# One ring of seven PSUM banks for the last 22 steps of a two-branch attention kernel, with its last projection units and row scaling moved

## The chip, the cores and the metric

The kernel runs on one core of a Trainium2 chip. The metric is device time in microseconds (us); the median of three runs before the change is 2747.71 us (2747.64 to 2748.46). Five engines work side by side and meet through semaphores: TensorE (PE, with its weight loads, PEld), VectorE (DVE), ScalarE (ACT), GpSimd (POOL), and SyncE (SP), which issues transfers. TensorE's results land in PSUM, which has eight banks of 128 x 512 f32; a bank may be written again only when its reader is done with it.

## The reference, cut to what matters

Two attention blocks read the same `x` (2048 x 576), each with 32 heads of 18 columns; in block B all heads share one key and one value head. A gate per row mixes the two.

```python
g = _sigmoid((x * gate_w).sum(-1, keepdims=True))
a = _A_ref(x, A_wqkv, A_wo)      # 32 heads, each with its own k and v
b = _B_ref(x, B_wq, B_wk, B_wv, B_wo)   # 32 heads, one k and one v
return g * a + (1 - g) * b
# in each: scores = q k^T * 18 ** -0.5;  p = softmax(scores);  o = p v;  heads joined;  o @ wo
```

## The kernel before, in words

There are 64 units (one per head; 0 to 31 are B's, 32 to 63 are A's). A unit has 16 steps, one per 128 keys, so the kernel has 1024 steps. A step has four scores matmuls (`step_scores`, L515; 128 keys x 512 queries each, one bank each), an exponential of each on ACT (L522, into one of 14 `pt` tiles), and the matmuls of probabilities and values (`step_pv`, L528; for the last unit `last_pv`, L539), which add into the eighth bank, `acc`. The scores run ahead of the value matmuls by two steps. The maxima that the exponentials subtract are found on DVE from a second set of scores (`step_max`, L471 and L480), 22 steps (`LEAD`) ahead. So from step 1002 on no maxima are left to find; this stretch is called the tail here. In it two scores matmuls of 56 rows stand on different halves of the PE array (`SB`, `MB`) and run beside each other.

The order of all instructions is written out by hand. `emit` reads a string of letters: `s` is one scores matmul, a digit n is n quarters of a step's value matmuls, `U` is the next unit of the output projection that waits in `todo`, `V` is the next unit of the last projection (`out_last`), and `a`, `b`, `c` are the three parts of `last_sums`, which brings half of the last unit's result into the rows of the last projection: a copy out of `acc`, a transpose (L710) with the division by the sums on DVE (L713 to L718), and transposes back (L724) with a split in a high and a low part (L115 to L119). A blank-separated stretch of a string such as "ss ss ss U 6" is called a group below.

The projection has three segments. The second (`SEG`, rows 512 to 1023 of the joined heads) gives 32 units of 12 matmuls (L677), each of which ends in one DVE addition (L686); 28 of them run before step 1002, and the last four in the tail. The third, `out_proj(8, [P])`, has 32 units of three matmuls; its rows come from the last heads and are scaled by `normalise(8, at_end=True)` (L612, L117, L119) in four chunks of 512 queries. Its units for queries 0 to 511 need chunk 0, and so on; four of its units are evicted by ACT and added by POOL (L683, L684), the others by DVE. Each finished pair of units sends a block of 128 rows to the output (L690).

Seven banks serve everything but `acc`: three of the pool `ps_s`, four of the pool `ps_m`. Before the change the tail's scores take two `ps_m` and two `ps_s` banks in turn, step by step, and the units and transposes take `ps_m` banks alone.

When a unit's value matmuls are done, `head_out` copies `acc` (L551) before the next unit's first value matmul may write it, and sends the sums and rows out. `normalise` for the last rows then waits for these sums, divides, multiplies by the gate, and brings the result back spread over partitions (`R`).

Of the kernel before, what the change touches and what calls it, by code (L numbers as in the profile page):

```python
# [8 lines left out]
F32 = mybir.dt.float32  # L9
# [3 lines left out]
OP = mybir.AluOpType  # L13
# [14 lines left out]
LEAD = 22  # L28
# [14 lines left out]
def gated_mix_kernel(ctx: ExitStack, tc: tile.TileContext, xT, wall, wv, wo, out):  # L43
    nc = tc.nc
    P = 128
# [7 lines left out]
    ps_s = ctx.enter_context(tc.tile_pool(name="ps_s", bufs=3, space=PSUM))  # L53
    ps_m = ctx.enter_context(tc.tile_pool(name="ps_m", bufs=4, space=PSUM))
# [34 lines left out]
    SB, MB = 0, 64  # L89
# [23 lines left out]
    def split(src, h, l, eng_h, eng_l):  # L113
        if eng_h is nc.scalar:
            nc.scalar.activation(h, src, AF.Copy)  # L115
        else:
            eng_h.tensor_copy(h, src)  # L117
        if l is not None:
            eng_l.tensor_tensor(l, src, h.bitcast(F32), op=OP.subtract)  # L119
# [224 lines left out]
    for n in range(4 * (LEAD_T - 3)):  # L344
        mt, c, w = next(left)
# [42 lines left out]
    L = {("kd", 0): kdb}  # L388
# [59 lines left out]
    def kst(u):  # L448
        return ksb if u < H else L["ks"][(u - H) % 3]
# [46 lines left out]
                    md.rearrange("(b i) (o a f) -> o a i b f", i=32, o=1, a=2)[:, a, 0:16])  # L496

    PT = {}

    def bank(n):  # L500

# [6 lines left out]

    def step_scores(u, i, c, alone, k):

        b = SB
        ps = (ps_m if alone and k < 2 else ps_s).tile([P, 512], F32, name="pm" if alone and k < 2 else "ps")
        if alone and k % 2:
            b = MB
        nc.tensor.matmul(ps, kst(u)[b:b + 56, i * P:(i + 1) * P],  # L515
                         qs[u % 3][b:b + 56, c * 512:(c + 1) * 512], start=True, stop=True)
        PT["q"] = PT.get("q", []) + [(c, ps)]
        if alone and k == 0:
            return
        for c, ps in PT.pop("q"):  # L520
            pt = L["pt"].tile([P, 512], F32, name="pt")
            nc.scalar.activation(pt, ps, AF.Exp, scale=SCALE)  # L522
            PT[u, i, c] = pt

    def step_pv(u, i, a, b):

        for j in range(4):
            nc.tensor.matmul(acc[32 * j:32 * j + 19, a:b], v_of(u, i), PT[u, i, j][:, a:b],  # L528
                             start=(i == 0), stop=(i == 15), skip_group_check=True)
        if b == 512:  # L530
            for j in range(4):
                del PT[u, i, j]

    def last_pv(half, i, a, b):

        for j in range(4):
            pt = PT[NU - 1, i, 2 * half + j // 2]
            x = 256 * (j % 2)
# [32 lines left out]
    def last_head(t):  # L571
        return (P * t + P - 1) // DH

    def normalise(t, at_end=False):

        u0 = 0 if t == 0 else last_head(t - 1) + 1
        u1 = min(last_head(t) + 1, NU - 1)
        rows = min(P, DH * (NU - 1) - P * t)
        off = FIRST_ROW[t]
        n = (u1 - u0) * 16  # L580
        sm = L["work"].tile([P, P], F32, name="sm", bufs=1)
        dma(sm[:n, :], sum_d[u0:u1, :].rearrange("h (s f) -> (h s) f", f=P))
        gt = L["work"].tile([P, P], F32, name="gt", bufs=1)
        dma(gt[:n, :], gu_d[u0:u1, :].rearrange("h (s f) -> (h s) f", f=P))
        yield
        yield

        g = P if t >= 7 else 32
        for c in range(0, P, g):
            nc.vector.reciprocal(sm[:n, c:c + g], sm[:n, c:c + g])  # L590
            yield
        (nc.vector if at_end else nc.gpsimd).tensor_tensor(sm[:n, :], sm[:n, :], gt[:n, :], op=OP.mult)
        dma(r_d[u0:u1, :].rearrange("h (s f) -> (h s) f", f=P), sm[:n, :])
        yield
        ot = OT.pop(t)
        R = L["work"].tile([P, S], F32, name="R", bufs=1)
        if off:
            nc.gpsimd.memset(R[0:32, :], 0.0)
        for cs in (slice(0, S // 2), slice(S // 2, S)) if at_end else (slice(0, S),):
            r0 = P * t  # L600
            while r0 < P * t + rows:
                u = r0 // DH
                n = min(DH * (u + 1), P * t + rows) - r0
                dma(R[off + r0 - P * t:off + r0 - P * t + n, cs], r_d[u:u + 1, cs].to_broadcast([n, cs.stop - cs.start]))
                r0 += n
        yield
        if at_end:
            L["end"] = {"h": qs[1], "l": L["ks"][2]}
            for c in range(4):
                cs = slice(512 * c, 512 * c + 512)  # L610
                e = nc.vector if c < 2 else nc.gpsimd
                e.tensor_tensor(ot[:, cs], ot[:, cs], R[:, cs], op=OP.mult)  # L612
                split(ot[:, cs], L["end"]["h"][:, cs], L["end"]["l"][:, cs], e, e)
            return
        for c in range(4):
            cs = slice(512 * c, 512 * c + 512)
            h = L["work"].tile([P, 512], F32R, name="oh", bufs=1)
            l = L["work"].tile([P, 512], F32R, name="ol", bufs=1)
            nc.gpsimd.tensor_tensor(ot[:rows, cs], ot[:rows, cs], R[:rows, cs], op=OP.mult)
            yield  # L620
            split(ot[:rows, cs], h[:rows], l[:rows], nc.gpsimd, nc.gpsimd)
            yield
            yield
            dma(on_d[0][P * t:P * t + rows, cs], h[:rows])
            dma(on_d[1][P * t:P * t + rows, cs], l[:rows])
            yield
# [19 lines left out]
    def out_proj(t0, rows, first=False):  # L646

        nt = len(rows)
        oacc = L["oacc"]
        fin = t0 == 8  # L650
        O = {}

        def load(q):
            for x, y in enumerate("hl"):
                if fin:
                    O[q, y] = L["end"][y][:, 256 * q:256 * q + 256].rearrange("p (t s) -> p t s", t=1)
                    continue
                t = L["pool"].tile([P, nt, 256], F32R, name=f"oi{y}", bufs=2)
                dma(t, on_d[x][P * t0:P * (t0 + nt), 256 * q:256 * q + 256]
                    .rearrange("(t p) s -> p t s", p=P))  # L660
                O[q, y] = t

        load(0)
        yield
        w = WO[t0]
        for q in range(8):
            if q < 7:
                load(q + 1)
            o = {y: O[q, y] for y in "hl"}
            for s2 in range(2):  # L670
                st_ = 2 * q + s2
                for hf in range(2):
                    ops = [(o[b][:r, t, s2 * P:(s2 + 1) * P], w[a][:r, t, 288 * hf:288 * hf + 288])
                           for a, b in PRODS for t, r in enumerate(rows)]
                    fp = ps_m.tile([P, 512], F32, name="pm")
                    for n, (x, y) in enumerate(ops):
                        nc.tensor.matmul(fp[:, 0:288], x, y, start=(n == 0), stop=(n == len(ops) - 1))  # L677
                    dst = oacc[:, st_, 288 * hf:288 * hf + 288]
                    if first:
                        nc.scalar.activation(dst, fp[:, 0:288], AF.Copy)  # L680
                    elif fin and hf == 0 and st_ in ON_ACT:
                        tmp = L["work"].tile([P, 288], F32, name="tmp", tag="ol", bufs=1)
                        nc.scalar.activation(tmp, fp[:, 0:288], AF.Copy)  # L683
                        nc.gpsimd.tensor_tensor(dst, tmp, dst, op=OP.add)  # L684
                    else:
                        nc.vector.tensor_tensor(dst, fp[:, 0:288], dst, op=OP.add)  # L686
                    if fin and st_ == 15:
                        dma(out[st_ * P:(st_ + 1) * P, 288 * hf:288 * hf + 288], dst)
                    elif fin and hf:
                        dma(out[st_ * P:(st_ + 1) * P, :], oacc[:, st_, :])  # L690
                    yield
# [5 lines left out]
    def last_sums(half):  # L697
# [7 lines left out]
        else:  # L705
            nc.vector.tensor_copy(oe[:, 0:256], acc[:, cols:cols + 256])
        yield
        pt = ps_m.tile([P, 512], F32, name="pm")
        for c in range(2):
            nc.tensor.transpose(pt[:, P * c:P * c + P], oe[:, P * c:P * c + P], ident)  # L710
        pt = pt[:, 0:256].rearrange("p (c j d) -> p c j d", c=2, d=32)
# [4 lines left out]
        ps = {}  # L716
# [2 lines left out]
                                    r[:, 2 * j:2 * j + 2].unsqueeze(2).to_broadcast([P, 2, DH]), op=OP.mult)  # L719
        yield  # L720
        for k in range(2):
            ps[k] = ps_m.tile([P, 512], F32, name="pm")
            for c in range(4):
                nc.tensor.transpose(ps[k][0:DH, P * c:P * c + P], on[:, 4 * k + c, 0:DH], ident)  # L724
        for k in range(2):
# [9 lines left out]
    NSTEP = 16 * NU  # L735
# [44 lines left out]
    for v in range(16):  # L780
        if v == 11:
            max_rows(0)
        mt, c, w = next(left)
        fp = ps_s.tile([P, 512], F32, name="ps")
# [20 lines left out]
    pos = {"s": 0, "P": 0, "x": (LEAD + 2) // 2, "y": (LEAD + 2) // 2}  # L805
# [76 lines left out]
    max_rows(NU - 1)  # L882


    for ops in ["ss ss ss U 6", "ss ss ss 6"] * 2 + ["ss ss ss U 6"] * 2 + ["ss ss ss 6"] * 5 + \
            ["a ss ss ss b 6 c", "ss ss ss 6 V V", "ss ss ss 6 V V", "ss ss V V 6 V V 6"]:
        emit(ops, 1)
    assert pos["s"] == pos["P"] == 4 * NSTEP
    emit("a V b V V c")
# [35 lines left out]
```

## Time and profile before

| What | Value |
|---|---|
| median of 3 runs | 2747.71 us |
| the profiled execution's own time | 2749.25 us |
| its span, first to last instruction | 2747.3 us |
| PE busy | 2732.3 us (99%) |
| DVE busy / ACT busy / POOL busy | 2394.7 / 2444.2 / 265.5 us |
| the tail: first paired scores to the last value matmul | 2671.25 to 2729.83 us |
| last DVE addition ends | 2742.84 us |

In the profile a row of the timeline gives the start in us, the length, engine, line, operation, output and inputs, how many instructions the row merges, and in brackets how long the engine had been idle before it and who ended that. A row of waits gives the sum of such idle time, how often it came, and the longest. Matmuls overlap, so the length of a row is longer than the time until the next matmul can start; the distance between starts is what a matmul costs its queue.

### The profile page before, as it was taken

What the parts mean: (1) busy time and instruction counts of PE and PEld (TensorE: products, weight loads), DVE (VectorE), ACT (ScalarE), POOL (GpSimd) and SP (SyncE); (2) the same over time, 40 slices, a digit from 0 to 9 for tenths busy, and PEclk for the clock granted to TensorE, in tenths of its full rate; (3) what the DMA queues carried; (4) which work ended last, traced back from release to release, by engine and by line L of the source; (5) the groups of instructions that cost most, each with busy time, mean ns of one, the idle gap of its engine ahead of it and who ended that gap; (6) DMA issues with size and microseconds to landing.
All of it is one profiled execution on the core that took longest, in us unless ns stands there. A gap on an engine that the chain in (4) does not pass through costs nothing.

```text
span 2747.3 us, 60434 instructions
## 1 busy us (share of the span) xinstructions
PE 2732.3 (99%) x23536; PEld 1301.3 (47%) x23536; DVE 2394.7 (87%) x4501; ACT 2444.2 (89%) x4787; POOL 265.5 (10%) x400
## 2 busy tenths in 40 slices
PE   9999999999999999999999999999999999999998
PEld 7874444454444333333334444444444333334555
DVE  4488888888889999999999898889889999998873
ACT  4338999999999999999999999999999999998776
POOL 2371000010001000100110001000100011011001
PEclk9999999999999999999999999999999999999999
DMA  8883211222111101211133223222321232233312
GB/s 285 325 300 125 59 50 40 61 79 74 43 57 57 56 26 34 65 48 31 47 98 104 87 61 92 91 77 67 101 86 56 59 91 91 66 97 102 111 36 87
DMA packets 145954, 242.09 MB, mean 88 GB/s; under 512 B 53650, under 2 KB 99810, under 8 KB 134092
## 3 DMA queue, kind: packets, MB, share of 16 engines
q1 hardware_dynamic: 131844, 188.16, 22.5%
q0 software_dynamic: 13504, 49.88, 4.8%
q8 instruction: 185, 3.03, 0.4%
q14 instruction: 101, 0.83, 0.1%
q10 hardware_dynamic: 320, 0.20, 0.0%
HBM read 149.61 MB, written 79.78 MB: 83 GB/s over the span
## 4 chain that ended last, share of the span: by engine, by line
PE 98%; ACT 1%; DMA 0%; issue 0%; DVE 0%; SPq 0%; ACTq 0%
PE acc L528 38%; PE ps L515 32%; PE pm L471 14%; PE ps L155 7%; PE pm L677 5%; PE pm L435 2%; ACT pt L522 1%; PE acc L539 0%; DMA wst<-wall 0%; PE ps L471 0%; PE pm L515 0%; DVE oacc L686 0%; PE pm L724 0%; PE pm L201 0%; SPq L49 0%
## 5 line engine op out<-in xcount | busy, mean ns | idle before, releaser
L522 ACT ACTIVATE pt<-ps 128x512 f32<-128x512 f32 x4052 | 2131.9, 611 | 124.2 <-PE pm L471 52.8
L480 DVE TENSOR_REDUCE mx<-pm 128x1 f32<-128x512 f32 x3064 | 1939.9, 684 | 195.0 <-PE pm L471 146.2
L515 PE MATMUL ps<-qs,ksb 56*128 56x512 f32 x2688 | 901.0, 437 | 0.6 <-DVE mx L480 0.3
L471 PE MATMUL pm<-ksb,qs 54*128 54x512 f32 x2332 | 793.4, 438 | 0.0
L515 PEld LDWEIGHTS ps<-qs,ksb 56*128 56x128 f32 x2688 | 435.8, 184 | 496.8 <-ACT pt L522 467.2
L528 PE MATMUL acc<-pt,vb 128*19 128x256 f32 (+3 forms) x6656 | 580.3, 435 | 0.1
L528 PE MATMUL acc<-pt,vg 128*19 128x256 f32 (+3 forms) x6232 | 554.2, 443 | 0.0
L515 PE MATMUL ps<-qs,ksa 56*128 56x512 f32 x1364 | 453.6, 436 | 3.9 <-ACT pt L522 3.8
L471 PEld LDWEIGHTS pm<-ksb,qs 54*128 54x128 f32 x2332 | 370.7, 185 | 124.5 <-DVE mx L480 57.0
L471 PE MATMUL pm<-ksa,qs 54*128 54x512 f32 x1232 | 425.6, 438 | 0.0
L477 DVE CUSTOM_DVE_ANT_0 junk<-pm,xb 128x512 bf16<-128x512 f32 x500 | 340.2, 680 | 1.1 <-ACT xb L474 0.9
L515 PEld LDWEIGHTS ps<-qs,ksa 56*128 56x128 f32 x1364 | 218.3, 184 | 243.5 <-ACT pt L522 225.5
L474 ACT ACTIVATE xb<-pm 128x512 f32<-128x512 f32 x500 | 307.3, 615 | 0.0
L528 PEld LDWEIGHTS acc<-pt,vb 128*19 128x19 f32 x6656 | 125.7, 97 | 216.6 <-issue 193.2
L471 PEld LDWEIGHTS pm<-ksa,qs 54*128 54x128 f32 x1232 | 198.0, 184 | 56.4 <-DVE mx L480 25.8
L528 PEld LDWEIGHTS acc<-pt,vg 128*19 128x19 f32 x6232 | 119.0, 97 | 207.0 <-issue 183.0
L117 POOL CAST mh<-mt 128x32 fp32r<-128x32 f32 x64 | 13.4, 210 | 1724.3 <-DVE mt L488 1724.3
L471 PE MATMUL pm<-kdb,qs 54*128 54x512 f32 x372 | 153.5, 413 | 0.0
L161 ACT ACTIVATE phl<-ps 128x512 fp32r<-128x512 f32 x40 | 23.9, 597 | 71.5 <-PE ps L155 57.0
L155 PE MATMUL ps<-xh,wh 128*128 128x512 f32 (+1 forms) x300 | 85.4, 383 | 0.6 <-ACT xh L274 0.3
L155 PE MATMUL ps<-xh,wl 128*128 128x512 f32 (+1 forms) x300 | 83.3, 376 | 0.0
L167 DVE TENSOR_TENSOR phl<-ps,phl 128x512 fp32r<-128x512 f32 x40 | 27.7, 692 | 62.7 <-ACT phl L161 47.2
(128 smaller groups left out, 1450.7 us busy)
## 6 DMA issues: line engine op xcount, KB each, us to landing
qs<-qk SPq DMA_DIRECT2D x384, 144.0 KB
qk<-phl POOLq DMA_DIRECT2D x56, 512.0 KB, 5.4
ksa<-qk SPq DMA_DIRECT2D x132, 144.0 KB
ksb<-qk SPq DMA_DIRECT2D x66, 144.0 KB
xv<-x_d SPq DMA_DIRECT2D x16, 576.0 KB
onh<-oh SPq DMA_DIRECT2D x32, 256.0 KB
onl<-ol SPq DMA_DIRECT2D x32, 256.0 KB
oih<-onh SPq DMA_DIRECT2D x16, 512.0 KB
```

Source lines behind the costliest of these rows:

```text
L155: nc.tensor.matmul(fp[:, p0:p0 + g], w[a][:kr, k, :], X[b][:kr, k, x0 + p0:x0 + p0 + g], start=(n == 0), stop=(n == len(PROJ) - 1))
L161: nc.scalar.activation(hl[:, 0, :], fp, AF.Copy)
L167: nc.vector.tensor_tensor(hl[:, 1, :], fp, hl[:, 0, :].bitcast(F32), op=OP.subtract)
L435: nc.tensor.matmul(fp[:, 0:288], x[:kr, k if b == "h" else NKT + k, :], w[hf][a][:kr, k, :], start=(n == 0), stop=(n == len(PROJ) - 1))
L471: nc.tensor.matmul(pm, qs[u % 3][b:b + 54, i * P:(i + 1) * P], k, start=True, stop=True)
L474: nc.scalar.activation(MX["x", u, i], pm, AF.Relu)
L477: nc.vector.tensor_tensor_reduce(junk, pm, MX.pop(("x", u, i)), 1.0, -3e38, op0=OP.add, op1=OP.max, accum_out=MX[u][:, i, c:c + 1])
L480: nc.vector.tensor_reduce(MX[u][:, i, c:c + 1], pm, axis=AX.X, op=OP.max)
L515: nc.tensor.matmul(ps, kst(u)[b:b + 56, i * P:(i + 1) * P], qs[u % 3][b:b + 56, c * 512:(c + 1) * 512], start=True, stop=True)
L522: nc.scalar.activation(pt, ps, AF.Exp, scale=SCALE)
L528: nc.tensor.matmul(acc[32 * j:32 * j + 19, a:b], v_of(u, i), PT[u, i, j][:, a:b], start=(i == 0), stop=(i == 15), skip_group_check=True)
L677: nc.tensor.matmul(fp[:, 0:288], x, y, start=(n == 0), stop=(n == len(ops) - 1))
```

## The change

Up to step 1002 the order of the instructions stays the same on every engine. From there on:

- A function `ring` hands out banks in the order s, m, s, m, s, m, m, so that scores, the second segment's last units, `last_sums` and the third segment's units all go round the same seven banks.
- The four `U` stand in groups 1, 4, 5 and 8 (counted from 0) and not in groups 0, 2, 4 and 5. Group 4 takes eight quarters of value matmuls and group 5 four, so that unit 62 ends with group 4. Group 10 has four scores and four quarters, and is followed by `a`. The eight `V` of the tail stand two each behind groups 12, 13 and 14 and one each before the last two stretches of four quarters.
- `normalise` at the end does all four chunks on POOL; before, DVE did chunks 0 and 1.

SP's order of transfers is the same. POOL gets six instructions more and DVE six fewer.

```diff
+    RING = [0]
+    def ring():
+        RING[0] += 1
+        m = RING[0] % 7 % 2
+        return (ps_m if m == 0 else ps_s).tile([P, 512], F32, name="ps" if m else "pm")
+
+    def unit_bank():
+        return ring() if pos["s"] > 4 * (NSTEP - LEAD) else ps_m.tile([P, 512], F32, name="pm")
...
     def step_scores(u, i, c, alone, k):
-        b = SB
-        ps = (ps_m if alone and k < 2 else ps_s).tile([P, 512], F32, name="pm" if alone and k < 2 else "ps")
-        if alone and k % 2:
-            b = MB
+        b = MB if alone and k % 2 else SB
+        ps = ring() if alone else ps_s.tile([P, 512], F32, name="ps")
...
             for c in range(4):
                 cs = slice(512 * c, 512 * c + 512)
-                e = nc.vector if c < 2 else nc.gpsimd
-                e.tensor_tensor(ot[:, cs], ot[:, cs], R[:, cs], op=OP.mult)
-                split(ot[:, cs], L["end"]["h"][:, cs], L["end"]["l"][:, cs], e, e)
+                nc.gpsimd.tensor_tensor(ot[:, cs], ot[:, cs], R[:, cs], op=OP.mult)
+                split(ot[:, cs], L["end"]["h"][:, cs], L["end"]["l"][:, cs], nc.gpsimd, nc.gpsimd)
...
-                    fp = ps_m.tile([P, 512], F32, name="pm")
+                    fp = unit_bank()
...
-        pt = ps_m.tile([P, 512], F32, name="pm")
+        pt = ring()
...
-            ps[k] = ps_m.tile([P, 512], F32, name="pm")
+            ps[k] = ring()
...
-    for ops in ["ss ss ss U 6", "ss ss ss 6"] * 2 + ["ss ss ss U 6"] * 2 + ["ss ss ss 6"] * 5 + \
-            ["a ss ss ss b 6 c", "ss ss ss 6 V V", "ss ss ss 6 V V", "ss ss V V 6 V V 6"]:
+    for ops in ["ss ss ss 6", "ss ss ss U 6", "ss ss ss 6", "ss ss ss 6", "ss ss ss U 8", "ss ss ss U 4",
+                "ss ss ss 6", "ss ss ss 6", "ss ss ss U 6", "ss ss ss 6", "ss ss 4 a", "ss ss ss b 6 c"] + \
+            ["ss ss ss 6 V V"] * 3 + ["V 4 V 4"]:
         emit(ops, 1)
```

## The prediction

> **What bounds the kernel now.** The page comes first, for its engines and its costliest groups; then the waits between 2671 and 2735 us, the only stretch that the change touches; then the chain that ended last; then the timelines of PE, ACT, DVE and POOL there.
>
> ```profile
> PE 2732.3 (99%) x23536; PEld 1301.3 (47%) x23536; DVE 2394.7 (87%) x4501; ACT 2444.2 (89%) x4787; POOL 265.5 (10%) x400
> ...
> L522 ACT ACTIVATE pt<-ps 128x512 f32<-128x512 f32 x4052 | 2131.9, 611 | 124.2 <-PE pm L471 52.8
> ```
>
> PE is busy throughout; an exponential lasts 0.61 us. With 15 us of idle in the whole span, PE can only give what it waits in the tail. The waits there:
>
> ```profile
> PE ps L515 <- ACT pt L522: 3.8, 7, 0.9
> ...
> PE acc L539 <- DVE oe L551: 0.9, 1, 0.9
> ...
> PE pm L677 <- ACT pt L522: 0.8, 3, 0.3
> ```
>
> Three lines, 5.5 us: scores that wait for a `ps` bank which an exponential still reads, one wait for the copy of `acc`, units that wait 0.3 each for a bank. The chain shows how one such wait ends:
>
> ```profile
> 2700.20 0.67 ACT pt L522
> ...
> 2700.91 0.49 PE ps L515
> ```
>
> The exponential ends at 2700.87, and 0.04 us later the score starts in its bank. PE's timeline gives the prices:
>
> ```profile
> 2671.25 0.51 PE L515 MATMUL pm<-qs,ksa 56*128 56x512 f32 x2
> ...
> 2692.44 0.81 PE L677 MATMUL pm<-woh,oih 128*128 128x288 f32 x4
> ...
> 2694.25 0.63 PE L528 MATMUL acc<-pt,vg 128*19 128x256 f32 x8
> 2695.74 1.06 PE L539 MATMUL acc<-pt,vg 128*19 128x256 f32 x16 [0.86 <-DVE oe L551]
> 2696.73 0.50 PE L515 MATMUL pm<-qs,ksa 56*128 56x512 f32 x2
> 2697.07 0.40 PE L515 MATMUL ps<-qs,ksa 56*128 56x512 f32 x2
> 2697.30 0.39 PE L515 MATMUL pm<-qs,ksa 56*128 56x512 f32 x2
> 2697.62 1.49 PE L539 MATMUL acc<-pt,vg 128*19 128x256 f32 x24
> 2699.04 0.50 PE L515 MATMUL ps<-qs,ksa 56*128 56x512 f32 x2
> ...
> 2700.91 0.49 PE L515 MATMUL ps<-qs,ksa 56*128 56x512 f32 x1 [0.91 <-ACT pt L522]
> 2701.34 1.49 PE L539 MATMUL acc<-pt,vg 128*19 128x256 f32 x24
> ...
> 2713.40 0.44 PE L710 MATMUL pm<-ident,oe 128*128 128x128 f32 x2
> 2713.76 1.49 PE L539 MATMUL acc<-pt,vg 128*19 128x256 f32 x24
> 2715.19 1.04 PE L724 MATMUL pm<-ident,on 128*18 128x128 f32 x8
> 2716.16 0.50 PE L515 MATMUL pm<-qs,ksa 56*128 56x512 f32 x2
> ...
> 2719.26 0.40 PE L677 MATMUL pm<-woh,qs 128*128 128x288 f32 x1
> ...
> 2720.26 0.50 PE L515 MATMUL ps<-qs,ksa 56*128 56x512 f32 x2
> ...
> 2729.83 0.40 PE L677 MATMUL pm<-woh,qs 128*128 128x288 f32 x1
> ...
> 2730.33 0.62 PE L710 MATMUL pm<-ident,oe 128*128 128x128 f32 x2
> ...
> 2734.20 0.38 PE L677 MATMUL pm<-woh,qs 128*128 128x288 f32 x1 [0.68 <-DVE ksb L119]
> ```
>
> By starts: pairs of scores cost 0.34, 0.23 and 0.32; six quarters of values 1.42 (2697.62 to 2699.04), 0.237 each; so a group without a wait costs 2.31. A `U` adds 1.81, `V V` 1.00, one `V` 0.50, `b` 0.36, `c` 0.97. A score that has lost its partner to a wait costs 0.43 more (2700.91 to 2701.34).
>
> ```profile
> 2697.32 1.08 ACT L522 ACTIVATE pt<-pm 128x512 f32<-128x512 f32 x2 [1.29 <-PE pm L515]
> ...
> 2702.11 1.21 ACT L522 ACTIVATE pt<-ps 128x512 f32<-128x512 f32 x2
> ```
>
> Twelve exponentials, the first ending at 2697.93 and the last at 2703.32: 0.49 apiece, and the first starts 0.59 after its score. Six cost ACT 2.94, more than a bare group's 2.31 and less than a group with `U`, 4.12. So PE and ACT take turns as the limit, and the banks between them decide how much is lost at each turn.
>
> The 15 groups last from 2671.25 to 2729.83, 58.58 us. Their bare work is 4 x 4.12 + 7 x 2.31 + 3.64 (with `b` and `c`) + 2 x 3.31 + 5.51 = 48.4. **Lost: 10.2 us**; the listed waits are the visible part, the rest is pairs taken apart.
>
> **The change, part by part.**
>
> *Ring and new places of the units.* The bare work stays: 6 x 2.31 + 4 x 4.12 (8 and 4 quarters make up for 6 and 6) + 1.62 + 3.64 + 3 x 3.31 + 2.90 = 48.4. For the loss I carry three rules through the new order: PE goes in order at the prices above; an exponential ends 0.49 after the one before, or 1.20 after its score's start if that is later; a bank is free 0.04 after its reader. Groups 0 and 1 as the example: exponentials 0 to 5 end at 2672.45, then every 0.49, so number 4 at 2674.41 and 5 at 2674.90. Group 0 runs bare to 2673.56. In group 1 the first two pairs find banks; at 2674.13 the sixth score, the ring's twelfth, needs the bank of exponential 4, comes apart from its partner and goes at 2674.45; `U` takes the next bank, free at 2674.94. The group costs 4.6 and not 4.12: 0.50 lost. The same way: groups 0, 2, 5, 6, 9, 10, 13, 14 and the last run bare, since a group with `U` lets ACT catch up; group 3 loses 0.50, group 4 0.61, 7 0.50, 8 0.62, 11 0.88. Group 12 loses 1.35: its sixth score gets the bank of its own second one, whose exponential is still queued. Sum 4.96. The same rules give 10.5 for the old order, where the trace has 10.2, so I take 4.8. The copy of `acc` no longer stalls PE: unit 62 ends with group 4, and group 5's scores and `U`, 2.7 us, stand over it, against 0.86. **Gain 10.2 - 4.8 = 5.4.** Ends: all loss gone, 10.2; the groups keep the lengths that they have, below, 1.8. I take the worked sum, as the rules give the old order within 0.4. Alternating `ps` and `pm` costs nothing between ends of 0: both kinds of rows last 0.39 to 0.51. The last four units load nothing, so no transfer moves.
>
> *After the last value matmul.* The wait of 0.68 at 2734.20 is for one of the two banks of `c`, fourth-last of four; in a ring of seven it is not asked for until five units later. What is late next is DVE and then the output:
>
> ```profile
> 2734.73 2.49 DVE L686 TENSOR_TENSOR oacc<-pm,oacc 128x288 f32<-128x288 f32 x6
> ...
> 2740.79 2.05 DVE L686 TENSOR_TENSOR oacc<-pm,oacc 128x288 f32<-128x288 f32 x5 [0.34 <-PE pm L677]
> ```
>
> ```profile
> 2738.00:2740.00 2.00, 2.00 (x17) 2.00 (x16) 1.66 (x6) 0.41 (x1) 1.19 (x2) 1.00 0.64 240
> 2740.00:2742.00 2.00, 2.00 (x17) 2.00 (x16) 1.66 (x6) 0.41 (x1) 0.96 (x2) 1.00 1.03 388
> ```
>
> DVE's 17 additions at 0.415 from 2734.73 end at 2741.8 if PE is never late, against 2742.84: 1.0. The transfer engines stand at a share of 0.64 in one 2 us stretch and 1.03 in the next, so they can take in 0.36 x 2, some 0.7, more. I take **0.8**, between the two (ends 0 and 1.0).
>
> *POOL alone.* The price is two chunks more on POOL.
>
> ```profile
> 2711.78 1.76 POOL L612 TENSOR_TENSOR ot<-ot,R 128x512 f32<-128x512 f32 x1 [38.00 <-PE ps L515]
> ...
> 2715.53 1.28 POOL L612 TENSOR_TENSOR ot<-ot,R 128x512 f32<-128x512 f32 x1
> ...
> 2717.57 1.29 POOL L119 TENSOR_TENSOR ksb<-ot,qs 128x512 fp32r<-128x512 f32 x1
> ```
>
> ```profile
> 2694.99 0.69 DVE L551 COPY oe<-acc 128x512 f32<-128x512 f32 x1 [0.18 <-PE acc L528]
> ...
> 2708.74 0.69 DVE L612 TENSOR_TENSOR ot<-ot,R 128x512 f32<-128x512 f32 x1 [6.22 <-DMA R<-r_d]
> ...
> 2715.83 0.68 DVE L117 CAST qs<-pm 18x512 fp32r<-18x512 f32 x1 [1.01 <-PE pm L724]
> ...
> 2717.15 0.67 DVE L117 CAST qs<-pm 18x512 fp32r<-18x512 f32 x1
> ```
>
> A chunk lasts 3.33 (2715.53 to 2718.86) to 3.75. `R`'s first half comes 13.75 after the copy, which now stands at 2688.5: 2702.3, and chunk 1 ends by 2709.8 at the longer price. Its first reader is DVE's second cast in `c`, 1.96 after `c` starts (2717.15 against 2715.19); `c` starts at about 2709.6, so 2711.5. Chunk 0 has 4 us, chunks 2 and 3 over 10. The cover is 1.7 us; beyond it each microsecond stops DVE, and PE with it. Cost 0. DVE, freed of its 3.6 us, was waiting there anyhow: 0.
>
> That margin is where a rule weighs. POOL's first product took 1.76 while DVE multiplied two SBUF tensors, and 1.28 later. The Trainium skill, SBUF — State Buffer, Who interferes with whom, says a VectorE instruction with two SBUF inputs contends with a GpSimd one that reads SBUF, and one with at most one does not; the trace agrees. By it the new order, where DVE's neighbours read PSUM, gives 3.33 a chunk and chunk 1 at 2709.0; by the longer row, 2709.8: the sum is the same, the late-POOL rival loses chance.
>
> **Sum.** 5.4 + 0.8 = 6.2 us. The profiled execution took 2749.25, of which 2747.3 is its span; it would become 2743.05 with a span of 2741.1. It lies 1.5 above the median of the runs, 2747.71; against that median, **2741.5**.
>
> **The rivals.**
>
> *The ring does not help.* Groups stay as now: without `U` 3.01 on average (two of them from 2696.73 to 2701.34 + 1.42), with `U` 4.12 and 0.3 of wait. Then 6 x 3.01 + 17.7 + 2.0 + 4.6 + 4.1 + 2 x 3.7 + 2.9 = 56.8, a gain of 1.8 + 0.8, **2745.1**. For it: two groups without `U` are already 98% ACT (2.94 of 3.01). Against it: the lost time sits at the groups with `U`, the copy and `c`.
>
> *POOL late.* Decided when a chunk takes over 4.6 us. At twice its length, 6.7, chunk 1 comes 4 us late and PE loses some 3.5: **2745.0**. For it: the margin is small. Against it: no chunk row is over 3.75.
>
> *The ring takes pairs apart (slower).* Each score waits for its own exponential, and these end 0.49 apart, so pairs may part everywhere, not once a group. Then a group is 6 x 0.43 + 1.42 = 4.0; the tail is about 73, a loss of 14: **2761**. Each parted pair costs about 0.4: from 16 more than I count the change is no gain, from 30 (of 44) it is slower by over 0.2%. For it: in the trace the pair that meets a busy bank always parts. Against it: bare work is 48.4 against ACT's 43, so PE mostly comes late and finds banks free.
>
> **How the numbers follow.** 0.2%, 5.5 us, is about what a measurement of this kernel tells from no change. Forecast 0.65 (range of its own 2739.2 to 2743.0), ring no help 0.20, POOL late 0.08, pairs apart 0.07. The forecast's part above 5.5 gives faster 0.58; the rest of it and the first two rivals are within 0.2%, 0.35; slower 0.07. Above 2745.5 lie the third rival and part of the others, below 2739.2 the case that most of the loss goes (bound: 10.2 + 1.0, 2736.5): 2739.2 to 2745.5.
>
> **What would show it.** Right: the copy of `acc` near 2688.5 with no PE wait behind it; PE's waits for exponentials in the tail under 2 us in sum, most in groups with `U` and in group 12; the last value matmul near 2724.4; no wait behind `c`; POOL's four chunks at about 3.3 each and no DVE wait for them. Wrong: second scores that stand alone throughout, a DVE cast that waits for POOL, an output that ends no earlier than DVE allows.

## The result, and the profile after

| | before | after |
|---|---|---|
| median of 11 runs | 2747.93 us | 2741.99 us (2740.39 to 2742.36) |
| ratio, 95% interval | | 0.9976 [0.9967, 0.9985] |
| profiled execution, and its span | 2749.25, 2747.3 us | 2740.89, 2739.1 us |
| the tail: first paired scores to the first instruction behind the last value matmul | 58.58 us, from 2671.25 | 52.92 us, from 2670.11 |
| from there to the end of the last DVE addition | 13.01 us | 11.79 us |

The two medians are 5.9 us apart, against 6.2 forecast. The two profiled executions are 8.4 apart, and their spans 8.2: 5.66 of that is the tail, 1.22 the stretch behind it, 0.2 the output (its end lies 3.6 to 4.7 behind the last addition in the ten traces of this document), and 1.14 lies ahead of the tail, where both kernels issue the same instructions. That last part is scatter (the run of the kernel before alone, below), and is not counted.

The page of the kernel after: engines with busy time, share of the span and instructions; the line of the exponentials.

```profile
PE 2730.7 (100%) x23528; PEld 1299.5 (47%) x23528; DVE 2391.4 (87%) x4495; ACT 2443.3 (89%) x4787; POOL 271.2 (10%) x406
...
L530 ACT ACTIVATE pt<-ps 128x512 f32<-128x512 f32 x4048 | 2133.1, 612 | 121.3 <-PE pm L471 52.3
```

Work is the same on PE and ACT; what moved is when it could start. (The eight PE instructions fewer are value matmuls, L528 and now L536: eight quarters in one group go as four and four, where six and the next two went as four, two and two.) PE's waits in the tail and behind it are down to one line, from five (sum in us, times, longest):

```profile
PE pm L523 <- ACT pt L530: 0.7, 1, 0.7
```

PE's timeline of the kernel after, from the tail's start to the first instruction behind the last value matmul (start, length):

```profile
2670.11 0.50 PE L523 MATMUL ps<-qs,ksa 56*128 56x512 f32 x1
...
2679.83 0.39 PE L523 MATMUL ps<-qs,ksa 56*128 56x512 f32 x1
2680.09 0.49 PE L523 MATMUL pm<-qs,ksa 56*128 56x512 f32 x1
2680.51 1.49 PE L536 MATMUL acc<-pt,vg 128*19 128x256 f32 x16
...
2689.82 1.06 PE L547 MATMUL acc<-pt,vg 128*19 128x256 f32 x16
...
2707.99 1.04 PE L731 MATMUL pm<-ident,on 128*18 128x128 f32 x8
2708.96 0.50 PE L523 MATMUL ps<-qs,ksa 56*128 56x512 f32 x1
...
2709.53 0.39 PE L523 MATMUL ps<-qs,ksa 56*128 56x512 f32 x1
2710.63 0.50 PE L523 MATMUL pm<-qs,ksa 56*128 56x512 f32 x1 [0.72 <-ACT pt L530]
2711.06 1.49 PE L547 MATMUL acc<-pt,vg 128*19 128x256 f32 x24
...
2722.04 1.06 PE L547 MATMUL acc<-pt,vg 128*19 128x256 f32 x16
2723.03 0.40 PE L684 MATMUL pm<-woh,qs 128*128 128x288 f32 x1
```

Three things are to be seen. The first value matmuls after the copy of `acc` (2689.82) carry no wait, where before they had 0.86. The one wait left is the sixth score of group 12 (2710.63). And most of what is still lost shows as no wait at all: at 2680.09 the sixth score starts 0.26 after its partner instead of beside it, and the value matmuls follow 0.42 behind it (2680.51). That it waits for its bank is seen on ACT. The first and the fifth exponential of the tail of the kernel after are:

```profile
2670.65 0.60 ACT L530 ACTIVATE pt<-ps 128x512 f32<-128x512 f32 x1 [0.56 <-PE pm L523]
...
2672.57 0.63 ACT L530 ACTIVATE pt<-ps 128x512 f32<-128x512 f32 x1
```

The fifth ends at 2673.20, and the sixth score of group 1, which is the twelfth of the ring and needs that bank, starts at 2673.26, 0.25 after its partner. A parted score counts as busy time. The view by windows shows it: the whole tail in each kernel, its length and each engine's busy time.

```profile
2671.25:2729.83 58.58, 52.59 (x518) 27.61 (x515) 14.74 (x33) 44.50 (x88) 8.98 (x9) 1.00 0.12 38
```

```profile
2670.11:2723.03 52.92, 52.20 (x510) 27.38 (x506) 11.75 (x27) 44.08 (x88) 14.76 (x15) 1.00 0.13 42
```

PE (first column after the length) is busy 52.6 us before and 52.2 after, though the same work needs 48.4 when every pair runs side by side; TensorE's granted clock is 1.00 in both.

The stretch behind the tail, DVE's timeline of the kernel after:

```profile
2727.93 0.43 DVE L693 TENSOR_TENSOR oacc<-ps,oacc 128x288 f32<-128x288 f32 x1
2728.30 1.16 DVE L693 TENSOR_TENSOR oacc<-pm,oacc 128x288 f32<-128x288 f32 x3
2729.39 0.43 DVE L693 TENSOR_TENSOR oacc<-ps,oacc 128x288 f32<-128x288 f32 x1
...
2732.76 0.46 DVE L693 TENSOR_TENSOR oacc<-pm,oacc 128x288 f32<-128x288 f32 x1 [0.34 <-PE pm L684]
...
2734.36 0.46 DVE L693 TENSOR_TENSOR oacc<-pm,oacc 128x288 f32<-128x288 f32 x1
```

The last 17 additions take 6.89 us (2727.93 to 2734.82); before they took 8.11 (2734.73 to 2742.84). They start 4.90 after the end of the tail in both.

### The profile page after: what moved, and what is told of

Read it like the earlier page. It is cut to its first block, busy times and chain, and to the rows that moved or that the text cites. A ratio compares the mean times of both kernels' runs of the same rounds, so it can differ in the third digit from the quotient of the medians.

```text
span 2739.1 us, 60392 instructions
## 1 busy us (share of the span) xinstructions
PE 2730.7 (100%) x23528; PEld 1299.5 (47%) x23528; DVE 2391.4 (87%) x4495; ACT 2443.3 (89%) x4787; POOL 271.2 (10%) x406
## 4 chain that ended last, share of the span: by engine, by line
PE 99%; DMA 0%; ACT 0%; DVE 0%; issue 0%; ACTq 0%
PE acc L536 38%; PE ps L523 32%; PE pm L471 15%; PE ps L155 6%; PE pm L684 4%; PE pm L435 2%; PE acc L547 1%; PE pm L523 0%; DMA xsh<-xT 0%; PE ps L471 0%; PE ps L684 0%; DMA wst<-wall 0%; ACT pt L530 0%; DVE oacc L693 0%; PE pm L731 0%; PE pm L201 0%
## 5 line engine op out<-in xcount | busy, mean ns | idle before, releaser
L536 PE MATMUL acc<-pt,vb 128*19 128x256 f32 (+3 forms) x6656 | 580.2, 434 | 0.1
L536 PE MATMUL acc<-pt,vg 128*19 128x256 f32 (+3 forms) x6224 | 553.9, 443 | 0.1
L536 PEld LDWEIGHTS acc<-pt,vb 128*19 128x19 f32 x6656 | 125.4, 97 | 216.7 <-issue 193.2
L536 PEld LDWEIGHTS acc<-pt,vg 128*19 128x19 f32 x6224 | 118.6, 97 | 207.8 <-issue 183.8
```

## The experiments

"Tail" and "end" are the two stretches of the table above, read from each kernel's trace; a median stands against runs of the kernel before on the same chip.

| kernel | median us (runs) | ratio to before, 95% | tail | end | PE waits in the tail |
|---|---|---|---|---|---|
| before (profile; medians 2747.93 to 2748.22) | | | 58.58 | 13.01 | 5.97 |
| before, run again | 2748.06 (1) | | 58.52 | 13.01 | 5.96 |
| ring alone | 2743.19 (11) | 0.9984 [0.9975, 0.9993] | 54.76 | 11.80 | 1.94 |
| order alone | 2747.69 (11) | 0.9998 [0.9989, 1.0007] | 57.79 | 13.01 | 4.88 |
| POOL alone, nothing else | 2747.84 (11) | 0.9999 [0.9990, 1.0008] | 59.39 | 12.99 | 6.36 |
| after | 2741.99 (11) | 0.9976 [0.9967, 0.9985] | 52.92 | 11.79 | 0.72 |
| after, chunks 0 and 1 on DVE | 2742.57 (11) | 0.9979 [0.9970, 0.9988] | 53.88 | 11.79 | 1.46 |
| after, old banks behind the tail | 2742.68 (11) | 0.9979 [0.9971, 0.9988] | 53.22 | 12.99 | 0.89 |
| after, group 12 changed | 2740.81 (6) | 0.9970 [0.9958, 0.9982] | 52.24 | 11.80 | 0 |
| ring with an evened order | 2738.34 (5) | 0.9961 [0.9949, 0.9974] | 48.51 | 12.40 | 0 |

**The kernel before alone.** No edit; the question is how far the place of the tail moves from one execution to the next.

> The kernel before once more, for a second profile. The two traces of before and after differ by 1.1 us where the tail starts, though the instructions up to there are the same. Theory: that is scatter between executions, so this trace's tail starts between 2669.5 and 2672 us, lasts 58.6 us and is followed by 13.0 us to the last DVE addition. Rival: the change makes the part ahead of the tail faster, and the start stays at 2671.2 or later.

The tail starts at 2671.16 (2671.25 in the first profile), its length agrees within 0.06. Over all the traces, whose instructions ahead of the tail are the same, it starts between 2670.25 and 2671.25 on the old banks and between 2669.68 and 2672.04 with the ring, so the rival falls. Lengths inside the tail are compared below to a tenth of a microsecond, as far as one repeated trace bears that out; spans only to about 2 us.

**The ring alone.** The new banks with the old order and the old work on DVE and POOL.

```diff
+    def ring(): ...            # and unit_bank(), as in the change
-        ps = (ps_m if alone and k < 2 else ps_s).tile(...)
+        ps = ring() if alone else ps_s.tile(...)
-                    fp = ps_m.tile(...)
+                    fp = unit_bank()
-        pt = ps_m.tile(...)
+        pt = ring()
-            ps[k] = ps_m.tile(...)
+            ps[k] = ring()
```

> The old order of groups and the old sharing of the four chunks between DVE and POOL, with the ring of seven for all banks of the tail. Theory (the banks give the gain): carried through with the three rules of the prediction the tail lasts 54.2 us, against 58.6 before and 52.9 after; the wait of 0.8 for the copy of acc in group 5 stays, the waits of single ps scores go; behind the last value matmul no wait of 0.68; in all 5.5 to 6 us faster than before. Rival (the new places of the units give it): the tail stays near 58 us and the whole is at most 1.5 us faster than before.

The tail falls by 3.8 and the end by 1.2, 5.0 together, and so does the median (2748.22 to 2743.19). The rules gave a tail of 54.2; it is 54.76, with one wait in it that the rules leave out, the second line here. PE's waits:

```profile
PE acc L547 <- DVE oe L559: 0.9, 1, 0.9
PE pm L718 <- DVE oe L714: 0.9, 1, 0.9
PE ps L523 <- ACT pt L530: 0.2, 1, 0.2
```

The waits for exponentials sink from 3.8 + 0.8 + 0.5 to 0.2. The wait for the copy of `acc` stays, as the old order says. A wait that the kernel before did not have is the second line: the transposes of `b` wait 0.86 for a copy on DVE. DVE's timeline of the same kernel says why:

```profile
2705.36 0.69 DVE L620 TENSOR_TENSOR ot<-ot,R 128x512 f32<-128x512 f32 x1 [6.36 <-DMA R<-r_d]
...
2708.34 0.69 DVE L119 TENSOR_TENSOR ksb<-ot,qs 128x512 fp32r<-128x512 f32 x1
2708.95 0.42 DVE L714 COPY oe<-acc 128x256 f32<-128x256 f32 x1
```

DVE stands 6.36 us in its queue for `R`, then works off its two chunks, and the copy that PE needs comes behind them. In the kernel before, the copy ended at 2712.75, 0.65 ahead of the transposes. Counted from the tail's start, the transposes are ready 3.8 us earlier here (38.3 against 42.15) and `R` only 2.4 (35.05 against 37.5), so the chunks on DVE are now in the way. The ring was put in for the scores, the units and the transposes at once; which of them gains most inside the tail, no run separates.

**The order alone.** The new strings on the old banks.

```diff
-    for ops in ["ss ss ss U 6", "ss ss ss 6"] * 2 + ...
+    for ops in ["ss ss ss 6", "ss ss ss U 6", ... "ss ss 4 a", "ss ss ss b 6 c"] + \
+            ["ss ss ss 6 V V"] * 3 + ["V 4 V 4"]:
```

> The new order of groups with the old banks (two ps_m and two ps_s in turn, units and transposes in ps_m) and the old sharing between DVE and POOL. Theory: the tail lasts 58.5 us by the same rules, 0.5 less than they give for the order before; the copy of acc no longer stalls PE, but single ps scores still wait, 1 us in each of groups 1, 3 and 7; 0 to 1 us faster than before. Rival (the order gives the gain): 5 us faster.

```profile
PE ps L515 <- ACT pt L522: 3.8, 7, 0.9
PE pm L677 <- DVE ksb L119: 0.7, 1, 0.7
PE pm L677 <- ACT pt L522: 0.6, 2, 0.3
PE pm L515 <- ACT pt L522: 0.5, 1, 0.5
```

The new places of the units take the wait for `acc` away and little else: the first line is the same 3.8 us in seven waits as before, with 0.9 in each of groups 1, 3 and 7 as expected. The tail is 0.8 shorter in the trace (57.79), which is about what the order brings on top of the ring (0.9, below); the median falls by 0.5, which its interval doesn't tell from nothing. So the ring is the cause of most of the gain, and the order is worth under a microsecond with it or without it.

**POOL alone, nothing else.** All four chunks on POOL, the old order and the old banks.

```diff
-                e = nc.vector if c < 2 else nc.gpsimd
-                e.tensor_tensor(ot[:, cs], ot[:, cs], R[:, cs], op=OP.mult)
-                split(ot[:, cs], ..., e, e)
+                nc.gpsimd.tensor_tensor(ot[:, cs], ot[:, cs], R[:, cs], op=OP.mult)
+                split(ot[:, cs], ..., nc.gpsimd, nc.gpsimd)
```

> The kernel before with all four chunks of the last rows on POOL and nothing else. Theory: POOL's chunks are hidden and DVE was waiting anyhow, so within 0.7 us of before; chunks at 3.3 us each, since no DVE product of two SBUF tensors runs beside them. Rival (freeing DVE matters): 1.5 us or more faster, with the copy L706 and the transposes of last_sums earlier. Rival (POOL late): DVE's casts in c wait for POOL and the run is 2 us or more slower.

The median is the same within its interval, the tail 0.8 longer. Half of that is one wait, which no other kernel on the old banks has; DVE's, POOL's and PE's timelines, in this order:

```profile
2713.07 1.24 DVE L713 TENSOR_TENSOR rl<-rl,gl 128x8 f32<-128x8 f32 x1
```

```profile
2713.00 1.28 POOL L119 TENSOR_TENSOR ksb<-ot,qs 128x512 fp32r<-128x512 f32 x1
```

```profile
2714.59 1.04 PE L723 MATMUL pm<-ident,on 128*18 128x128 f32 x8 [0.38 <-DVE on L717]
```

A product of 128 x 8 numbers takes 1.24 us instead of 0.17. It started 0.07 after an instruction of POOL that reads two SBUF tensors, and ended 0.03 after that one's end. More on this below. The other half is a pair of scores in the next group that comes apart here and not in the kernel before (PE's timelines, before and here); why it does, these rows don't say:

```profile
2717.35 0.56 PE L515 MATMUL pm<-qs,ksa 56*128 56x512 f32 x2 [0.45 <-ACT pt L522]
```

```profile
2716.75 0.99 PE L515 MATMUL pm<-qs,ksa 56*128 56x512 f32 x2 [0.46 <-ACT pt L522]
```

**After, chunks 0 and 1 on DVE again.** What POOL alone is worth on top of the ring and the order.

```diff
-                nc.gpsimd.tensor_tensor(...)       # all four chunks
+                e = nc.vector if c < 2 else nc.gpsimd
+                e.tensor_tensor(...)
```

> The kernel after with chunks 0 and 1 back on DVE. DVE then stands at the first product until R lands, with the addition of the unit of group 8 queued behind it. Theory: that bank is held about 5 us longer; by the rules the tail is 0.6 us longer than after (53.5), so 0 to 1.5 us slower than after and still 4.5 to 6 us faster than before. Rival (POOL alone is a needed part of the gain): 3 us or more slower than after.

The tail is 0.96 longer, the median 0.6 higher (0.3 when each is taken against its own runs of the kernel before); the intervals of the two ratios overlap, so only the trace tells them apart. PE's timeline there:

```profile
2706.58 0.49 PE L523 MATMUL pm<-qs,ksa 56*128 56x512 f32 x1 [0.31 <-ACT pt L530]
...
2707.56 0.50 PE L523 MATMUL pm<-qs,ksa 56*128 56x512 f32 x1 [0.48 <-ACT pt L530]
...
2710.26 1.03 PE L732 MATMUL pm<-ident,on 128*18 128x128 f32 x8 [0.42 <-DVE on L726]
```

and DVE's:

```profile
2701.78 0.69 DVE L620 TENSOR_TENSOR ot<-ot,R 128x512 f32<-128x512 f32 x1 [6.08 <-DMA R<-r_d]
...
2705.37 0.45 DVE L694 TENSOR_TENSOR oacc<-pm,oacc 128x288 f32<-128x288 f32 x1
2705.73 0.42 DVE L714 COPY oe<-acc 128x256 f32<-128x256 f32 x1
...
2708.70 1.18 DVE L722 TENSOR_TENSOR rl<-rl,gl 128x8 f32<-128x8 f32 x1
```

Again DVE stands for `R` (6.08 us). The addition of group 8's unit, which starts at 2699.29 in the kernel after, waits behind the chunks until 2705.37, and its bank is held until then. That this bank is what the two waits in group 11 come from is argued; they are put down to ACT, and no run separates them. The third wait, 0.42 at 2710.26, comes from DVE's product L722, which takes 1.18; a fourth, of 0.25 in group 12, is for DVE's L119.

**After, old banks behind the tail.** The ring only up to the last value matmul.

```diff
     def unit_bank():
-        return ring() if pos["s"] > 4 * (NSTEP - LEAD) else ps_m.tile(...)
+        return ring() if 4 * (NSTEP - LEAD) < pos["s"] and pos["P"] < 4 * NSTEP else ps_m.tile(...)
-        pt = ring()
+        pt = unit_bank()
-            ps[k] = ring()
+            ps[k] = unit_bank()
```

> The kernel after, with the units, the transposes and the banks of last_sums that stand behind the last value matmul back in the four ps_m banks; the tail itself keeps the ring. Theory (the end gains by the banks alone): the tail stays at 52.9 us, the stretch from the last value matmul to the end of the last DVE addition goes from 11.8 back to 13.0 us with the wait of about 0.7 behind c, and the whole is 1.0 to 1.3 us slower than after. Rival (the end gains because POOL and DVE are done earlier): the end stays near 11.8.

```profile
2729.63 0.37 PE L684 MATMUL pm<-woh,qs 128*128 128x288 f32 x1 [0.68 <-DVE ksb L119]
```

The old wait behind `c` is back with its old length, and the end is 12.99, as before the change. So the 1.2 us of the end are the banks behind the last value matmul; POOL and DVE were done about as early as in the kernel after, and the end did not gain by it. The tail is 0.3 longer than after's, of which 0.18 is a wait for DVE's product `rl` (last section). Together the trace is 1.5 longer; the medians say 0.5 to 0.7, less than the 1.0 to 1.3 expected, and their intervals overlap with after's.

**After, group 12 changed.** The score that waited gets four quarters ahead of it.

```diff
-            ["ss ss ss 6 V V"] * 3
+            ["ss ss 4 ss 2 V V"] + ["ss ss ss 6 V V"] * 2
```

> The kernel after with group 12 written as four scores, four quarters, two scores, two quarters, V V. Theory (the sixth score of group 12 loses time because its bank is that of the group's own second score): the wait of 0.72 and the parted pair go, one more change between scores and values costs about 0.2; group 12 takes 3.5 us and not 4.4 to 4.5, the whole is 0.8 to 1.1 us faster than after. Rival (the wait only moves to the next groups, since ACT is the limit there): groups 13 to 15 grow by as much and nothing is gained.

PE's timeline of that group:

```profile
2710.84 0.40 PE L523 MATMUL pm<-qs,ksa 56*128 56x512 f32 x1
2711.17 1.06 PE L547 MATMUL acc<-pt,vg 128*19 128x256 f32 x16
2712.16 0.50 PE L523 MATMUL ps<-qs,ksa 56*128 56x512 f32 x1
2712.17 0.50 PE L523 MATMUL pm<-qs,ksa 56*128 56x512 f32 x1
```

The last two scores go side by side and wait for nothing. The group takes 3.66 (2710.50 to 2714.16) against 4.52, nearly the 3.5 expected, and groups 13 and 14 keep their lengths within 0.03, so the loss did not move on. The tail is 0.68 shorter, less than the 0.8 to 1.1 expected, in part since `c` ahead of the group starts 0.12 later (last section). The medians are 1.2 apart, with intervals that overlap. The same work in another order, within one group, took away PE's last wait of the tail.

**The ring with an evened order.** A bare group has six scores and 2.31 us of PE work, less than the 2.94 of their exponentials; a group with `U` has far more. Here units and quarters are spread so that, by the three rules of the prediction, PE's work keeps nearer to ACT's 0.49 per exponential at every point and a score seldom finds the ring full.

```diff
-    for ops in ["ss ss ss 6", "ss ss ss U 6", ... ["ss ss ss 6 V V"] * 3 + ["V 4 V 4"]:
+    for ops in ["ss ss 2", "ss ss 8", "ss ss ss 2 U", "ss ss 6", "ss ss ss 6", "ss 6", "ss ss ss 2 U",
+                "ss ss ss 8", "ss ss ss 8", "ss ss U", "ss ss ss 8", "ss ss ss 8 a", "ss ss ss 2 U b",
+                "ss ss ss 2 c 6", "ss ss ss 8 V V", "ss ss V V V V 2", "ss ss ss V 8 4 V"]:
```

> The kernel after with the order of the tail evened out: groups with U get two quarters or none, groups without get up to eight, so that each has about as much PE work as its six exponentials take ACT (2.9 us); the fourth U stands behind a, and V come in stretches of two to four. Theory (what is left of the loss, 4.5 us, is PE and ACT taking turns): by the three rules the tail takes 49.4 us, 4 us less than the same rules give for after; the whole is 3 to 4 us faster than after. Rival (the rest of the loss is the cost of changes between kinds of matmul and cannot be ordered away): less than 1 us faster, since the order has as many changes.

The first quarter of the tail by windows, in the kernel with the evened order and, in the second fence, in the kernel after:

```profile
2669.70:2681.80 12.10, 12.10 (x118) 5.45 (x118) 0.63 (x2) 11.56 (x24) 2.20 (x3) 1.00 0.04 7
```

```profile
2670.10:2683.30 13.20, 13.20 (x110) 6.16 (x106) 0.66 (x2) 11.91 (x25) 2.20 (x3) 1.00 0.04 7
```

PE is recorded as busy all the time in both; ACT is busy 96% of the time here and 90% there. The numbers of matmuls (118 and 110) don't compare, since quarters are written two or four to a matmul; work by the prices does. From 2669.68 to 2681.48, 11.80 us, the evened order does 13 pairs of scores, 24 quarters and a `U`, some 11.7 us of bare work. From 2670.11 to 2683.51, 13.40 us, the kernel after does 15 pairs, 24 quarters and a `U`, 11.9 us.

The tail is 48.51, where the rules gave 49.4, with no wait of PE in it. One `V` (0.50) now stands behind the last value matmul, so it compares with 47.9 of bare work; 0.6 is still lost. That unit and a wait of 0.24 for a copy stand in the end instead, which is 12.40 and not 11.8. The rival falls: the order has as many changes between kinds of matmul, and most of the loss went. At 2738.34 this version is below both kernels: 3.65 below the kernel after, and the intervals of the two ratios overlap only from 0.9967 to 0.9974.

## Why the prediction was right

The forecast, 2741.5 with a range of 2739.2 to 2745.5, stands against 2741.99. The range holds the times of the first two rivals too (2745.1 and 2745.0), so the time alone would not show the mechanism; its steps do:

**The bound and the three rules** held. The loss in the tail went from 10.2 to 4.5 (52.92 - 48.4), forecast 4.8. Group by group (from each group's start to the next one's, less its bare work):

| group (from 0) | 1 | 3 | 4 | 7 | 8 | 11 | 12 | all others together |
|---|---|---|---|---|---|---|---|---|
| loss forecast | 0.50 | 0.50 | 0.61 | 0.50 | 0.62 | 0.88 | 1.35 | 0 |
| loss measured | 0.38 | 0.36 | 0.62 | 0.36 | 0.68 | 0.74 | 1.21 | 0.13 |

Each loss sits in the group where it was forecast. Most terms were sized a little too large, since banks came free a little earlier than the rules had it: the fifth exponential ended 3.09 after the tail's start and not 3.16 (2673.20; exponentials in a row start 0.48 apart, the rule had 0.49). A parted score then costs a group 0.36 and not 0.50 (group 3: 2.67 against 2.31). The reason given for group 12 is in the trace, where ACT works on that group's second score from 2709.99 to 2710.58 and the sixth starts at 2710.63, and the run that changes only that group takes the loss away. One limit is not among the rules, the 14 `pt` tiles: ACT waited for them once in the tail, 0.6 us for the value matmuls of group 1, and PE shows no wait from it.

**The copy of `acc`** stands at 2687.29 with no PE wait behind it. It was forecast for 2688.5, counted from a tail that starts at 2671.25; from the tail's own start it is 17.18 against 17.25.

**The end** was sized at 0.8 and measured 1.22. The mechanism is shown by the run with the old banks there. Two things in the working were off. The 17 additions were counted at 0.415; in a row they come 0.36 to 0.41 apart (three from 2728.30, the next at 2729.39), 6.89 with a wait of 0.34 in it. And the output was taken as a brake because the transfer engines were shown full in one stretch; from the last addition to the end of the span it took 4.30, before 4.48, and 3.59 in the kernel before run again.

**POOL alone, cost 0**: the chunks were hidden as forecast, but two of the reasons were wrong. First, the chunks were on time with more room than forecast:

```profile
2704.18 1.29 POOL L619 TENSOR_TENSOR ot<-ot,R 128x512 f32<-128x512 f32 x1
...
2706.23 1.28 POOL L119 TENSOR_TENSOR ksb<-ot,qs 128x512 fp32r<-128x512 f32 x1
```

A chunk takes 3.28, chunk 1 ends at 2707.51, and the second cast of `c` starts at 2710.02: 2.5 us of room against 1.7. (That cast is no reader of chunk 1: it writes 18 rows of the same columns, `qs`, and has to come behind POOL's.) But "DVE's neighbours read PSUM" overlooked one that does not, the product in `b` (SBUF times SBUF, 128 x 8). It took 0.62 beside POOL and not 0.17; PE did not feel it, `c` starting right at the end of the value matmuls (2707.99). In three of the other kernels PE waited for it: 0.18, 0.38 and 0.42. Second, "freed of its 3.6 us, DVE was waiting there anyhow: 0" holds on the old banks only. With the ring, DVE's stand for `R` delays what PE needs, and taking the chunks off it is worth 1.0 in the tail's trace: this is the term that was mis-sized, and it is hidden in the 5.4, whose rules had no DVE stall in them: with the chunks left on DVE, the loss is 5.5 where 4.8 was forecast. So the same edit costs 0.8 of the tail where it stands alone and brings 1.0 where the ring has moved everything else forward.

**The shares.** By medians, each against its own runs of the kernel before: the ring 5.0; on top of it the order 0.6 and POOL alone 0.3; without the ring the order 0.5 and POOL alone 0.4. None of these but the ring's is told from nothing by a measurement of this kernel. By traces: 5.0 for the ring (3.8 + 1.2), 0.9 for the order and 1.0 for POOL on top of it, 6.9 in all, where the medians give 5.9 and the forecast had 6.2. The difference of 1 us between the two readings is within the intervals and stays unexplained, so that the median ends this near to the forecast is in part luck: by the traces the tail was worth 0.3 and the end 0.4 more than worked out. Without the ring, the order brings 0.8 by the traces and POOL alone costs 0.8.

**The rivals.** That the ring does not help is refuted by the ring alone. Pairs taken apart everywhere would be a tail of 73; single scores stand alone in seven groups, once or twice each. POOL late did not come to pass; that DVE was the one held up by POOL was in none of the rivals.

## What to carry to other kernels

Where two engines hand buffers to each other and take turns as the limit, count the buffers as one ring: splitting the same seven banks by kind of work cost 5 us here, of which the one reordering tried on the old banks brought back under 1. Then carry three or four durations of the trace through the new order by hand, group by group; it tells where the rest is lost, and the order that evens it out was worth another 3.7. Look at starts and not at busy time: a matmul that has lost its partner counts as busy, so PE stood at 52.2 busy of 52.9 us with 4.5 us of loss in them.

## What the runs showed of the hardware

How long POOL holds up DVE can be read to a few hundredths. The product `rl<-rl,gl` of DVE has both inputs in SBUF. With POOL idle it takes 0.17 (2724.43 in the kernel after). Where it started under an instruction of POOL that reads SBUF, DVE's product lasted until that one's end and 0.02 to 0.03 longer, whatever was left of it:

| kernel | DVE's product | length | POOL's instruction |
|---|---|---|---|
| before, run again | 2713.98 to 2714.21 | 0.23 | cast, 2713.58 to 2714.19 |
| after | 2706.92 to 2707.54 | 0.62 | 2706.23 to 2707.51 |
| after, group 12 changed | 2708.34 to 2709.16 | 0.82 | 2707.85 to 2709.14 |
| after, old banks behind the tail | 2708.85 to 2709.80 | 0.95 | 2708.49 to 2709.77 |
| after, chunks on DVE | 2708.70 to 2709.88 | 1.18 | 2708.57 to 2709.86 |
| POOL alone, nothing else | 2713.07 to 2714.31 | 1.24 | 2713.00 to 2714.28 |

POOL's instruction, which had started first, kept its length (1.26 to 1.30, the cast 0.61). Five of them read two SBUF tensors; the first reads one, and holds the product all the same, in the one case that shows it (POOL's and DVE's timelines of the kernel before, run again):

```profile
2713.58 0.61 POOL L117 CAST qs<-ot 128x512 fp32r<-128x512 f32 x1
```

```profile
2713.98 0.23 DVE L714 TENSOR_TENSOR rl<-rl,gl 128x8 f32<-128x8 f32 x1
```

In the kernels where the product took 0.17 beside POOL, it started ahead of POOL's next instruction or met only its last 0.09 to 0.13, which its own length covers. In the kernel before, at the chunks, it was the other way round: POOL's product started 0.06 after DVE's of two SBUF tensors (2711.72), and POOL's was the longer one (1.76). The Trainium skill, SBUF — State Buffer, Who interferes with whom, says that such a pair contends and that the order of issue decides who blocks; the traces agree in both directions. Where the Trainium skill says there that a DVE instruction with at most one SBUF input does not contend, it sets DVE's two-port modes aside, a condition that the prediction leaves out; nothing in its sum turned on it.

PE feels it with the length. From the start of the last six quarters ahead of it, `c` starts after 1.42 at a length of 0.62, 1.54 at 0.82, 1.68 at 0.95, 1.91 at 1.18 and 1.87 at 1.24. So a small instruction on the path can cost seven times its time, by a neighbour that is not on the path.
